# Hash-masked attention and SwiGLU on one core: when the weights are loaded, when two head pairs are hashed, and which engine moves one head's bits

## The chip, the cores and the metric

The kernel runs on one core of a Trainium2 chip, in one launch. The metric is the device time of one execution in microseconds. The time before is the median of three runs; beside it stands one execution taken by the hardware profiler, from which all durations come.

## The reference

Four batches of eight heads, 768 tokens, 64 channels per head. Every query and key is hashed with six projections to six bits; a query sees only the keys with the same six bits. The result goes through an RMS norm and a SwiGLU layer (512 to 1536 to 512 channels).

```python
q_bits = (np.einsum('bhsd,dk->bhsk', q, proj) > 0)
k_bits = (np.einsum('bhsd,dk->bhsk', k, proj) > 0)
mask = q_bucket[:, :, :, None] == k_bucket[:, :, None, :]
scores = np.where(mask, scale * np.matmul(q, k.transpose(0, 1, 3, 2)), -1000000000.0)
attn = softmax(scores); x = attn @ v            # heads side by side: (3072, 512)
xn = x / rms * rms_g
out = (silu(xn @ w_gate) * (xn @ w_val)) @ w_out
```

## The kernel before, in words

**Bits as channels.** A head's queries and keys lie transposed in a tile `QK` with 70 partitions: 64 channels and 6 rows with the hash signs, scaled so that a pair of tokens with equal bits gains a constant that the exp's bias (`EBIAS`) takes off again. So one matmul of 70 rows gives masked scores, and a head's scores cannot start before its six bit rows lie in `QK`.

**Getting a pair of heads ready** (batch 0; `hp` is the pair, `hh` the head in it):

- `load_natural` and `load_v` load q, k and v by DMA from SP's queue (384 KB each).
- `turn_pe` (L141) transposes one head's q or k on TensorE into a PSUM bank `t_ps`; VectorE (DVE) copies it to `qT` or `kT` (L150).
- `cast_pool` (L186, `cast_part` L161) casts both to fp16 into `QK` on GpSimd (POOL).
- `hash_direct` (L230) multiplies with the projections (`d_ps`, L222); `sign` lets DVE write the sign bits of all four tensors of the pair to a tile `bits` (L211); `send` copies them to rows 64 to 69 of `QK` with four DMAs of 9 KB on SP's queue (L251).
- `v_prep` (L277) casts v to fp16 into `vl`; `v_mean` (L290) sums v over the tokens with a matmul (`m_ps`), which DVE scales to `cvb`.

Head pair 0 of batch 0 is prepared in a prologue, its bits written straight to `QK` by DVE.

**Order of the work.** The time is cut into slots. A slot t issues the two score matmuls of the next block (`scores`, L305), the exp of block t on ScalarE (`probs`, L319), and then the functions that a dictionary `plan` lists for slot t, in the order in which they were listed. Three slots make one head for one half of the queries (a unit u: batch u // 2, half u % 2). The heads come in the order (0,0), (0,1), (1,0), (1,1), then heads 2 to 7 of unit 0, then heads 2 to 7 of unit 1, so heads 2 and 4 and 6 of batch 0 start at slots 12, 18 and 24. Each engine runs its instructions in the order of issue; slots hold no engine back, only data does.

```python
    for t in range(LAST):
        if t + 1 < LAST:
            scores(*head_of(t + 1))
        probs(*head_of(t))
        for f in plan[t]:
            f()
```

`av` (L328) multiplies a head's exps with v in two parts; `attn_out` (L344) adds `cvb`, divides (DVE, then POOL's `x` and `sq`), and `sumsq` sums the squares. From slot `TX` = 37 on unit 0 is normed (`norm`, `turn_x`), and from slot 38 `spread` deals out 48 pieces of gate and value matmuls (`feed`, L407 to L415: 12 feature tiles of 128 columns, each gate then value) over slots 38 to 47, and from slot 48 the output projections of the unit before.

**Weights.** `load_w` (L509) loads and casts a piece of a weight matrix with a DMA issued from POOL's queue. Gate and value come in two pieces of 256 input rows each (768 KB in fp16), planned for slots 3 and 7 (gate) and 12 and 16 (value); the output weights follow at slots 39 and 42. All gate and value pieces hold all 1536 columns.

**PSUM.** Three banks (`gps`) are passed round among `t_ps`, `d_ps`, `m_ps`, `x_ps`, `g_ps`, `v_ps` and `y_ps`; scores have two tiles of their own, `o_ps` one. The loads share eight buffers (`lpool`), so a load waits until the tile eight loads before it has been read.

Of the kernel before, what the change touches and what calls it, by code (L numbers as in the profile page):

```python
# [17 lines left out]
S = 768  # L18
D = 64
DMODEL = H * D  # L20
DFF = 1536
# [12 lines left out]
def kernel(  # L34
# [12 lines left out]
    nc = tc.nc  # L47
# [26 lines left out]
    wg = const.tile([128, 4, DFF], FP16, name="wg")  # L74
    wv = const.tile([128, 4, DFF], FP16, name="wv")
# [54 lines left out]
    KROWS = D + 6  # L130
    qT, kT, QK = {}, {}, {}
# [9 lines left out]
    def turn_pe(b, hp, hh, which, keep=nc.vector.tensor_copy, act=()):  # L141

        src = raw[b, hp][0 if which == "q" else 1][:, hh].rearrange(
            "p (j e) d -> p j (e d)", e=2
        )
        ps = bank("t_ps", [128, 3, 128])
        for j in range(3):
            nc.tensor.transpose(ps[:, j, :], src[:, j], ident)  # L148
        psf = ps.rearrange("p j t -> p (j t)")
        keep(turned(b, hp, which)[:, hh, :], psf)  # L150
        o = 0 if which == "q" else S
        for e in act:
            nc.scalar.copy(
                QK[b, 2 * hp + hh, "h"][0:64, o + e * HALF : o + (e + 1) * HALF],
                psf[64 * e : 64 * e + 64, :],
            )

    def turned(b, hp, which):
        return (qT if which == "q" else kT)[b, hp].rearrange("p (h c) -> p h c", h=2)
# [48 lines left out]
    def signs(dst, ps):  # L208

        upper = ps.bitcast(U16).rearrange("p (c two) -> p c two", two=2)[:, :, 1]  # L210
        nc.vector.tensor_scalar(  # L211
            out=dst.bitcast(U16), in0=upper, scalar1=SIGN, scalar2=BIT,
            op0=ALU.bitwise_and, op1=ALU.bitwise_or,
        )

    def hash_pairs(srcs):


        pss = [bank("d_ps", [128, HALF]) for _ in range(2)]
        for t, src in enumerate(srcs):  # L220
            for e in range(2):
                nc.tensor.matmul(  # L222
                    pss[e][32 * t : 32 * t + 32, :],
                    pj[64 * e : 64 * e + 64, 6 * e : 6 * e + 32],
                    src[64 * e : 64 * e + 64],
                    start=True, stop=True, tile_position=(64 * e, 32 * t),
                )
        return pss

    def hash_direct(b, hp, heads):  # L230


        where = [(which, hh) for hh in heads for which in "kq"]
        pss = hash_pairs([turned(b, hp, which)[:, hh, :] for which, hh in where])
        bt = spool.tile([128, S], FP16, name="bits")

        def sign(e):
            signs(bt[:, e * HALF : (e + 1) * HALF], pss[e])

        def direct(which, e):  # L240
            t = where.index((which, heads[0]))
            o = (0 if which == "q" else S) + e * HALF
            signs(
                QK[b, 2 * hp + heads[0], "h"][D:KROWS, o : o + HALF],
                pss[e][32 * t : 32 * t + 6],
            )

        def send():
            for t, (which, hh) in enumerate(where):
                o = 0 if which == "q" else S  # L250
                nc.sync.dma_start(  # L251
                    out=QK[b, 2 * hp + hh, "h"][D:KROWS, o : o + S],
                    in_=bt[32 * t : 32 * t + 6, :],
                )

        return sign, direct, send

    def hash_one(b, hp):

# [45 lines left out]
    def scores(u, i):  # L305
        b, half = divmod(u, 2)
        h, ch = divmod(i, 3)
        ps = scps.tile([128, 2, 512], FP32, name="s_ps")
        for j in range(2):
            jt = 2 * ch + j  # L310
            nc.tensor.matmul(  # L311
                ps[:, j, 0:HALF],
                QK[b, h, "h"][0:KROWS, S + jt * 128 : S + (jt + 1) * 128],
                QK[b, h, "h"][0:KROWS, half * HALF : (half + 1) * HALF],
                start=True, stop=True,
            )
        sps[u, i] = ps
# [183 lines left out]
    def idle(n, new=None):  # L501

        ps = new("z_ps") if new else wz
        for _ in range(n):
            nc.tensor.matmul(ps, zeros16[:, 0:128], zeros16, start=True, stop=True)

    idle(8)

    def load_w(dst, src, kt, n):  # L509
        nc.gpsimd.dma_start(  # L510
            out=dst[:, kt : kt + n, :],
            in_=src[kt * 128 : (kt + n) * 128, :].rearrange("(k p) n -> p k n", p=128),
        )


# [7 lines left out]
    def at(w, s, f, *a):  # L523
        plan[NS * w + s].append(lambda: f(*a))
# [4 lines left out]
    cast_part(0, 0, "k", 1, 0, 1)  # L529
    turn_pe(0, 0, 1, "k")  # L530
    idle(1)
    _, direct, _ = hash_direct(0, 0, (0,))
    turn_pe(0, 0, 1, "q", nc.scalar.copy)
    idle(2)
    for which, e in (("k", 0), ("k", 1), ("q", 0)):
        cast_part(0, 0, which, e, 1, 1)
    for which, e in (("k", 0), ("q", 0), ("k", 1)):
        direct(which, e)
    scores(0, 0)
    _, direct1, _ = hash_direct(0, 0, (1,))  # L540


    def second_head():
# [2 lines left out]
        direct("q", 1)  # L546
        direct1("q", 1)

    pair_signs, sends = {}, {}

    def hash_only(b, hp):
        pair_signs[b, hp], _, sends[b, hp] = hash_direct(b, hp, (0, 1))

    def hash_signs(b, hp):
        for e in range(2):
# [2 lines left out]
    def hash_pair(b, hp):  # L558
        hash_only(b, hp)
        hash_signs(b, hp)  # L560

    def send_pair(b, hp):
        sends[b, hp]()

    at(0, 0, second_head)

    at(0, 1, cast_part, 0, 0, "q", 1, 0, 2, nc.vector)
    for hp, s0 in ((1, 2), (2, 7), (3, 13)):
        at(0, s0, new_pair, 0, hp)
        at(0, s0, turn_pe, 0, hp, 0, "k")  # L570
        at(0, s0 + 1, turn_pe, 0, hp, 1, "k")
        at(0, s0 + 1, cast_pool, 0, hp, "k")
        at(0, s0 + 2, turn_pe, 0, hp, 0, "q")
        at(0, s0 + 3, turn_pe, 0, hp, 1, "q")
        at(0, s0 + 3, cast_pool, 0, hp, "q")
        at(0, s0 + 4, hash_pair, 0, hp)
        at(0, s0 + 5, send_pair, 0, hp)
    at(0, 3, v_prep, 0, 0, nc.vector)
    at(0, 1, load_natural, nc.sync, 0, 3, "k")
    at(0, 1, load_natural, nc.sync, 0, 3, "q")  # L580
    at(0, 2, load_v, nc.sync, 0, 2)
# [1 line left out]
    at(0, 8, v_prep, 0, 1, nc.vector)  # L583
    at(0, 13, v_prep, 0, 2, nc.vector)
    at(0, 19, v_prep, 0, 3, nc.vector)
    for hp, t in enumerate((7, 18, 24, 30)):
        at(0, t, v_mean, 0, hp, 2, range(6))
    for i in range(2):
        at(0, 3 + 4 * i, load_w, wg, moe_w_gate, 2 * i, 2)
        at(0, 12 + 4 * i, load_w, wv, moe_w_val, 2 * i, 2)  # L590
        at(0, 39 + 3 * i, load_w, wo, moe_w_out, 6 * i, 6)


    for hp, ts in ((0, (8, 22, 23, 24, 25, 24, 26, 26, 28, 42)), (1, (12, 27, 28, 29, 30, 29, 41, 32, 33, 43))):
        tl, ts = ts[0], ts[1:]
        for w in "kq":
            at(0, tl, load_natural, nc.sync, 1, hp, w)
        at(0, tl, load_v, nc.sync, 1, hp)
        at(0, ts[0], new_pair, 1, hp)
        for t, hh, w in zip(ts[0:4], (0, 1, 0, 1), "kkqq"):  # L600
            at(0, t, turn_pe, 1, hp, hh, w)
        at(0, ts[4], cast_pool, 1, hp, "k")
        at(0, ts[5], cast_pool, 1, hp, "q")
        if hp == 0:
            at(0, ts[6], hash_pair, 1, hp)
            at(0, ts[7], send_pair, 1, hp)
        at(0, ts[8], v_prep, 1, hp)
        at(0, ts[8], v_sum, 1, hp)

    spots = {  # L610
        (1, 2): (20, (48, 48), (49, 49), 50),
        (1, 3): (45, (57, 57), (58, 59), 60),
        (2, 0): (50, (63, 64, 65, 66), (67, 69, 70, 71), 73),
        (2, 1): (62, (72, 73, 75, 81), (82, 83, 84, 85), 86),
# [16 lines left out]
    at(0, 24, nc.gpsimd.tensor_scalar_mul, gcol, gcol, float(DMODEL) ** 0.5)  # L631
    for n, (u, h) in enumerate(order):
        for part in range(2):
            at(0, 3 * n + 4 + part + (n == 0), av, u, h, part)
        if h % 2:
            if (u, h) == (0, H - 1):

                at(0, 3 * n + 5, o_step, u, h // 2, nc.vector)
                at(0, 3 * n + 5, s_step, u, h // 2)
                at(0, 3 * n + 5, norm_scale, u)  # L640
                at(0, 3 * n + 6, hash_only, 1, 1)
                at(0, 3 * n + 6, hash_signs, 1, 1)
                at(0, 3 * n + 6, norm, u)
                at(0, TX + 1, send_pair, 1, 1)
                at(0, TX - 1, idle, 2, bank)
                at(0, TX, idle, 1, bank)
                for c in range(3):
                    at(0, TX, turn_x, u, c, c == 1)
                continue
            at(0, 3 * n + 5, o_step, u, h // 2)  # L650
            at(0, 3 * n + (10 if h < 7 else 7), s_step, u, h // 2)
# [35 lines left out]
    for u in range(7):  # L687
# [11 lines left out]
        for i in range(9):  # L699
            c, n = divmod(i, 3)  # L700
# [12 lines left out]
    def behind_norm(t):  # L713

        return t - t % NS + 7 if 2 <= t % NS < 7 else t

    for (b, hp), (load, kturns, qturns, _) in spots.items():
# [7 lines left out]
        t = behind_norm(qturns[-1] + 2)  # L725
# [66 lines left out]
```

## Time and profile before

| | us |
|---|---|
| median of 3 runs (lowest to highest) | 349.69 (348.59 to 350.16) |
| the profiled execution | 348.41 |
| its span, first to last instruction | 346.5 |
| TensorE busy (PE) | 331.5 (96%) |
| VectorE busy (DVE) | 233.4 (67%) |
| ScalarE busy (ACT) | 224.3 (65%) |
| GpSimd busy (POOL) | 148.4 (43%) |
| mean granted TensorE clock | 0.99 |

Busy time counts what an engine computes; PEld is TensorE's weight load, which overlaps its matmuls. In the list of slices the span is cut into 40 equal parts of 8.66 us, and a digit is the busy share in tenths; PEclk is the clock that TensorE was granted, in tenths. The chain of waits is followed back from the last instruction, at each step to what released it. "QK<-bits" is the DMA of L251; "SPq" and "POOLq" are the queues from which DMAs are issued. A wait for several things is put down to the one that came last.

### The profile page before, as it was taken

The numbers are of one execution on the slowest core, as the hardware profiler recorded it, in microseconds if no ns is written. First come the engines' busy times: TensorE is split into PE (matmuls) and PEld (weight loads), VectorE is DVE, ScalarE is ACT, GpSimd is POOL, SyncE is SP. The second block draws the span as 40 slices with busy tenths as digits, with TensorE's granted clock in tenths as the row PEclk, the third lists the DMA queues.
The fourth block names the chain that finished last, engine by engine and source line by source line (L and its number), as shares of the span: only waits on it lengthen the run. The fifth ranks groups of instructions, "written<-read, shape, count | busy, mean of one in ns | idle before, by whom it ended". The sixth has DMA issues, their size and how long they took to land.

```text
span 346.5 us, 7807 instructions
## 1 busy us (share of the span) xinstructions
PE 331.5 (96%) x3004; PEld 199.0 (57%) x3004; DVE 233.4 (67%) x489; ACT 224.3 (65%) x325; POOL 148.4 (43%) x202
## 2 busy tenths in 40 slices
PE   8864999999999999999999999999999999999996
PEld 4443575665556646565656556565656556664554
DVE  3855478677688847985688846886586646675770
ACT  2854588666656766777677766777667776863322
POOL 3296272933762373465265533456371121112000
PEclk9999699999999999999999999999999999999999
DMA  7899870980363924443462415300200010001002
GB/s 242 273 187 279 221 138 12 165 153 33 50 153 62 164 75 116 98 66 78 99 136 43 100 65 98 75 3 5 80 17 5 1 62 32 0 2 61 33 0 91
DMA packets 78692, 30.94 MB, mean 89 GB/s; under 512 B 65000, under 2 KB 74688, under 8 KB 78656
## 3 DMA queue, kind: packets, MB, share of 16 engines
q1 hardware_dynamic: 75552, 25.47, 30.2%
q0 software_dynamic: 2656, 4.72, 7.7%
q8 instruction: 23, 0.38, 0.5%
q10 hardware_dynamic: 448, 0.27, 0.3%
q14 instruction: 13, 0.11, 0.1%
HBM read 28.32 MB, written 6.29 MB: 100 GB/s over the span
## 4 chain that ended last, share of the span: by engine, by line
PE 85%; DMA 4%; DVE 3%; ACT 1%; issue 1%; SPq 0%; DVEq 0%
PE v_ps L415 18%; PE g_ps L415 17%; PE y_ps L444 17%; PE s_ps L311 16%; PE o_ps L336 9%; DMA QK<-bits 4%; PE d_ps L202 3%; PE x_ps L398 2%; PE d_ps L222 1%; PE y_ps L463 1%; PE t_ps L148 1%; ACT psb L323 1%; DVE bits L211 1%; PE m_ps L296 1%; DVE a L432 0%
## 5 line engine op out<-in xcount | busy, mean ns | idle before, releaser
L323 ACT ACTIVATE psb<-s_ps,ebias 128x768 f16<-128x768 f32 x192 | 167.8, 899 | 34.4 <-PE s_ps L311 33.4
L311 PE MATMUL s_ps<-QK 70*128 70x384 f16 x384 | 94.7, 328 | 9.4 <-DMA QK<-bits 7.6
L423 ACT ACTIVATE t<-g_ps 128x384 f32<-128x384 f32 x96 | 47.1, 490 | 56.2 <-PE g_ps L415 56.0
L415 PE MATMUL g_ps<-xnT,wg 128*128 128x384 f16 x384 | 82.5, 325 | 0.2
L415 PE MATMUL v_ps<-xnT,wv 128*128 128x384 f16 x384 | 81.7, 325 | 0.2 <-DVE a L432 0.2
L432 DVE SCALAR_TENSOR_TENSOR a<-t,g_ps 128x384 f32<-128x384 f32 x96 | 52.7, 549 | 28.5 <-ACT t L423 27.1
L444 PE MATMUL y_ps<-wo,ht 128*128 128x512 f16 x276 | 68.0, 378 | 0.0
L357 POOL TENSOR_TENSOR x<-otmp,rcp 128x384 f32<-128x384 f32 x31 | 25.7, 829 | 97.3 <-DVE rcp L355 96.9
L336 PEld LDWEIGHTS <-psb 128*128 128x128 f16 x1152 | 52.4, 97 | 19.0 <-issue 4.3
L433 DVE SCALAR_TENSOR_TENSOR ht<-a,v_ps 128x384 f16<-128x384 f32 x96 | 53.2, 554 | 11.3 <-PE v_ps L415 3.1
L311 PEld LDWEIGHTS <-QK 70*128 70x128 f16 x384 | 34.9, 98 | 42.0 <-issue 11.6
L336 PE MATMUL o_ps<-vl,psb 128*128 128x65 f16 x1152 | 56.8, 193 | 0.5 <-DVE vl L280 0.5
L415 PEld LDWEIGHTS <-wv 128*128 128x128 f16 x384 | 35.2, 97 | 22.6 <-issue 1.8
L415 PEld LDWEIGHTS <-wg 128*128 128x128 f16 x384 | 34.7, 97 | 21.2 <-DVE xnT L404 0.6
L444 PEld LDWEIGHTS <-ht 128*128 128x128 f16 x276 | 24.7, 97 | 22.7
L362 POOL TENSOR_TENSOR sq<-x 128x384 f32<-128x384 f32 x31 | 25.6, 826 | 2.4
L194 POOL CAST QK<-kT 64x768 f16<-64x768 f32 x20 | 16.4, 820 | 22.6 <-DVE kT L174 7.7
L456 ACT COPY ysb<-y_ps 128x512 f32<-128x512 f32 x23 | 13.5, 585 | 18.6 <-PE y_ps L444 18.6
L350 DVE TENSOR_TENSOR otmp<-o_ps,cvb 128x390 f32<-128x390 f32 x32 | 17.9, 558 | 10.5 <-PE o_ps L336 10.4
L194 POOL CAST QK<-qT 64x768 f16<-64x768 f32 x20 | 16.5, 825 | 18.5 <-DVE qT L181 17.1
L366 DVE TENSOR_REDUCE ssp<-sq 128x3 f32<-128x384 f32 x32 | 16.9, 528 | 9.9 <-POOL sq L362 9.9
L211 DVE TENSOR_SCALAR bits<-d_ps 128x384 uint16<-128x384 uint16 x20 | 10.7, 553 | 14.2 <-PE d_ps L222 11.5
(70 smaller groups left out, 264.5 us busy)
## 6 DMA issues: line engine op xcount, KB each, us to landing
vn<-in_v_dram SPq DMA_DIRECT2D x16, 384.0 KB
out_dram<-ysb SPq DMA_DIRECT2D x23, 256.0 KB
qL<-in_q_dram SPq DMA_DIRECT2D x40, 96.0 KB
kL<-in_k_dram SPq DMA_DIRECT2D x40, 96.0 KB
kn<-in_k_dram SPq DMA_DIRECT2D x5, 384.0 KB
qn<-in_q_dram SPq DMA_DIRECT2D x5, 384.0 KB
wg<-in_moe_w_gate_dram POOLq DMA_DIRECT2D x2, 768.0 KB, 8.5
wv<-in_moe_w_val_dram POOLq DMA_DIRECT2D x2, 768.0 KB, 9.8
```

The lines of the kernel that those rows point to most:

```text
L194: nc.gpsimd.tensor_copy(QK[b, 2 * hp + hh, "h"][0:64, o : o + S], src[64 * hh : 64 * hh + 64, :])
L311: nc.tensor.matmul(ps[:, j, 0:HALF], QK[b, h, "h"][0:KROWS, S + jt * 128 : S + (jt + 1) * 128], QK[b, h, "h"][0:KROWS, half * HALF : (half ...
L323: nc.scalar.activation(psb[u, h][:, 2 * ch : 2 * ch + 2, :], sps.pop((u, i))[:, :, 0:HALF], AF.Exp, bias=ebias, scale=ESCALE,)
L336: nc.tensor.matmul(o[:, c, hh, 0:65], psb[u, h][:, jt, c * 128 : (c + 1) * 128], vls[b % 2][:, h, 2 * (jt % 3) + jt // 3 if b in PARITY el ...
L350: nc.vector.tensor_add(tmp[:, :, :, 0:65], o[:, :, :, 0:65], cvb[b % 2][:, 2 * hp : 2 * hp + 2, 0:65].unsqueeze(1).to_broadcast([128, 3, 2 ...
L357: eng.tensor_mul(xd.rearrange("p c (h d) -> p c h d", h=2), tmp[:, :, :, 0:64], r.to_broadcast([128, 3, 2, 64]),)
L362: eng.tensor_mul(sq, xd, xd)
L415: nc.tensor.matmul(ps, w[:, kt, fs], xnT[u][:, kt, :], start=(kt == 0), stop=(kt == 3))
L423: nc.scalar.activation(t, fbank[u, ft, "g_ps"], AF.Tanh, scale=0.5)
L432: nc.vector.scalar_tensor_tensor(out=a, in0=t, scalar=1.0, in1=g, op0=ALU.add, op1=ALU.mult)
L433: nc.vector.scalar_tensor_tensor(out=ht[u][:, ft, :], in0=a, scalar=0.5, in1=vv, op0=ALU.mult, op1=ALU.mult)
L444: nc.tensor.matmul(y, ht[u][:, ft, c * 128 : (c + 1) * 128], wo[:, ft, :], start=(ft == 0), stop=(ft == NF - 1),)
```

## The change

- `load_w` takes a range of columns. Gate and value now come in column halves: 768 columns of all 512 input rows, so feature tiles 0 to 5 and 6 to 11. They are planned for slots 20 (gate, first half), 23 (value, first half), 33 and 36.
- Pairs 2 and 3 of batch 0 are turned, cast, hashed and sent from slots 5 and 11 on, before from 7 and 13.
- Of pair 1 (heads 2 and 3) DVE copies head 2's bits to `QK` with two `tensor_copy` of 6 x 768 (`move`); head 3's still go by two DMAs.
- The second query half of pair 0 is cast on POOL at slot 1, before on DVE; v of pair 0 is cast on POOL at slot 1, before on DVE at slot 3. `v_mean` of pair 0 is at slot 4, before 7, and the first head's `av` one slot sooner.
- The loads of batch 1's pair 1 go from slot 12 to 17, those of pair 2 from slot 20 to 34.

```diff
-        def send():
+        def move(hh):
+            for which in "kq":
+                t, o = where.index((which, hh)), 0 if which == "q" else S
+                nc.vector.tensor_copy(
+                    QK[b, 2 * hp + hh, "h"][D:KROWS, o : o + S], bt[32 * t : 32 * t + 6, :]
+                )
+
+        def send(only=heads):
             for t, (which, hh) in enumerate(where):
+                if hh not in only:
+                    continue
                 o = 0 if which == "q" else S
...
-    def load_w(dst, src, kt, n):
+    def load_w(dst, src, kt, n, cols=slice(None)):
         nc.gpsimd.dma_start(
-            out=dst[:, kt : kt + n, :],
-            in_=src[kt * 128 : (kt + n) * 128, :].rearrange("(k p) n -> p k n", p=128),
+            out=dst[:, kt : kt + n, cols],
+            in_=src[kt * 128 : (kt + n) * 128, cols].rearrange("(k p) n -> p k n", p=128),
         )
...
-    at(0, 1, cast_part, 0, 0, "q", 1, 0, 2, nc.vector)
-    for hp, s0 in ((1, 2), (2, 7), (3, 13)):
+    at(0, 1, cast_part, 0, 0, "q", 1)
+    at(0, 1, v_prep, 0, 0)
+    for hp, s0 in ((1, 2), (2, 5), (3, 11)):
...
-        at(0, s0 + 5, send_pair, 0, hp)
-    at(0, 3, v_prep, 0, 0, nc.vector)
+        if hp == 1:
+            at(0, s0 + 5, send_pair, 0, hp, (1,))
+            at(0, s0 + 5, move_head, 0, hp, 0)
+        else:
+            at(0, s0 + 5, send_pair, 0, hp)
...
-    for hp, t in enumerate((7, 18, 24, 30)):
+    for hp, t in enumerate((4, 18, 24, 30)):
         at(0, t, v_mean, 0, hp, 2, range(6))
-    for i in range(2):
-        at(0, 3 + 4 * i, load_w, wg, moe_w_gate, 2 * i, 2)
-        at(0, 12 + 4 * i, load_w, wv, moe_w_val, 2 * i, 2)
+    for i, t in enumerate((20, 33)):
+        cols = slice(i * DFF // 2, (i + 1) * DFF // 2)
+        at(0, t, load_w, wg, moe_w_gate, 0, 4, cols)
+        at(0, t + 3, load_w, wv, moe_w_val, 0, 4, cols)
         at(0, 39 + 3 * i, load_w, wo, moe_w_out, 6 * i, 6)
-    for hp, ts in ((0, (8, ...)), (1, (12, 27, ...))):
+    for hp, ts in ((0, (8, ...)), (1, (17, 27, ...))):
...
-        (1, 2): (20, (48, 48), (49, 49), 50),
+        (1, 2): (34, (48, 48), (49, 49), 50),
...
-            at(0, 3 * n + 4 + part + (n == 0), av, u, h, part)
+            at(0, 3 * n + 4 + part, av, u, h, part)
```

## The prediction

> **What bounds the kernel now.** The page comes first: the slices of the span.
>
> ```profile
> PE   8864999999999999999999999999999999999996
> PEclk9999699999999999999999999999999999999999
> DMA  7899870980363924443462415300200010001002
> ```
>
> From the seventh slice (52 us) on TensorE is full, and its clock is full too; only slices 1 to 5 (8.7 us each) have room. The change edits the plan of slots 0 to 38 (one slot is one block of scores and its exp), and slot 38, the first gate matmul, starts at 58.74 us. So I cost those 58.74 us; the 287.8 us behind them are the same TensorE work in nearly the same order and count at nothing. Next, stretches of those slices:
>
> ```profile
> 17.20:21.80 4.60, 4.56 (x70) 3.71 (x62) 3.67 (x9) 3.34 (x5) 4.38 (x7) 1.00 0.85 161
> 21.80:24.50 2.70, 0.09 (x4) 0.01 (x1) 0.74 (x2) 0.36 (x1) 2.54 (x4) 1.00 1.08 215
> 24.50:30.20 5.70, 5.61 (x76) 3.91 (x76) 3.91 (x9) 4.54 (x6) 2.95 (x5) 1.00 1.06 292
> 30.20:35.10 4.90, 0.00 (x0) 0.00 (x0) 0.62 (x2) 0.45 (x1) 4.68 (x6) 0.82 1.08 254
> 35.10:40.20 5.10, 5.05 (x45) 2.55 (x46) 1.87 (x5) 2.01 (x3) 0.06 (x1) 0.50 1.09 295
> 40.20:58.70 18.50, 17.82 (x243) 12.24 (x240) 14.64 (x32) 16.25 (x23) 9.29 (x12) 1.00 0.42 82
> ```
>
> The columns are length, busy PE, PEld, DVE, ACT, POOL, granted clock, DMA share. TensorE stands still twice while the DMA engines are full, and after the second stop it runs 5 us at half clock. Who is waited for is in the chain of waits of that stretch, and in the list of waits:
>
> ```profile
> 19.51 4.88 DMA QK<-bits
> ...
> 27.73 7.28 DMA QK<-bits
> ...
> 35.95 1.46 PE d_ps L222 x16
> ```
>
> ```profile
> PE s_ps L311 <- DMA QK<-bits: 7.6, 2, 5.0
> ```
>
> The scores of heads 2 and 4 wait 2.63 us (to 24.52) and 4.96 us (to 35.15) for their six rows of hash bits, which L251 copies from SBUF to SBUF by DMA, 9 KB each. The timeline of the issues says why they are late: the gate and value quarters leave POOL's queue at 17.21, 19.86, 25.91 and 34.40, the bits leave SP's at 18.60 and 26.98. In the trace's packet records the first gate quarter (256 rows of 3072 bytes, 247 ns each, 16 on each DMA engine) moves from 18.94 to 23.8, and the first bits move at 22.98; the next bits come out from 33.0 on, behind batch 1's loads and the first value quarter (30.0 to 36.2).
>
> **The change part by part.** *Weights behind the bits* (plan, `load_w`). Until slot 18 no weights are under way. That removes A = 2.63 and B = 4.96, if nothing else is late there. *Clock.* With B goes the half clock. From 35.15 to 39.96 the chain holds 4.81 us of matmuls; the same groups elsewhere in it at full clock: scores 0.48, hash 0.94, o_ps 0.38, then 0.33, 0.35 and 0.33 make 2.81, so C = 2.0. *Value cast and av one slot sooner.* `v_prep` (0,0) goes from DVE (15.14) to POOL, idle from 9.73 to 15.17 (vn had landed by 9.9; the q cast and it are two POOL casts of some 0.83): the 0.49 us that o_ps waits for vl ends, D = 0.5, and DVE loses two casts of 0.56. If that cover went, pair 1's k casts behind them would be late, with 4 us to spare before slot 11. Ceiling: 2.63 + 4.96 + 2.0 + 0.5 = 10.1 us.
>
> *Head 2's bits by DVE.* Two copies of 6 x 768 fp16 replace two DMAs of SP (0.66 to 0.85 us of its queue each). No row shows an fp16 copy inside SBUF; bounds are the 128x128 CAST, 0.23, and the 64x768 CAST, 0.56. I take 0.4, between them (same length as the second, half its bytes). They sit on DVE in front of pair 2's q copies. What is queued: from 10.71 five sign ops (2.76), four t_ps copies of pair 1 (0.51 apart), cvb 0.28, signs 1.02, two moves 0.8, four copies of pair 2: 8.9, to which come waits for turns and hash as before (0.92 + 0.47) and some 0.4 of drain, so pair 2's hash can start at about 21.4 and the scores behind it at 22.5; without the stop TensorE would have been there at 21.9. Head 2 itself is ready near 19.3. *Pairs 2 and 3 two slots sooner.* Same number of turns, casts and hashes; the pace is DVE's. Between the hashes of pairs 2 and 3 DVE has 1.02 + 4 x 0.51 + v_prep 0.56 + ssp 0.54 + otmp and rcp 0.75 = 4.9 us, TensorE 6 x 0.33 + 4 x 0.27 + 4 x 0.33 + 0.94 = 5.3, so here only the copy behind the last turn shows. Together E = 1.3: 0.6 for the first hash and 0.7 for the second, which the second stop hid; bounds 0 (DVE gap-free) and 3.9 (rival 2).
>
> By the Trainium skill (SBUF — State Buffer, "Who interferes with whom") a VectorE copy in a two-port mode and a GpSimd operation exclude each other. The trace agrees: a POOL cast beside the vl cast at 15.14 took 1208 ns instead of 823. By the page alone each move could wait a whole cast.
>
> *Do the later DMAs meet their users?* Pair 2's bits (sent near 23.5) go behind batch 1's first loads, issued after slot 8 (near 20.5, 3 x 384 KB; such a load took about 1.15 us while the queue was alone, before 14 us): landed by 27, wanted near 29. Pair 3's are sent near 30 and wanted from 34. Behind them SP issues pair (1,1)'s loads, now slot 17, near 33; POOL, which nothing holds until its slot, sends the first gate half near 31, when pair 3's casts and x, sq are done. Loads issued beside weights before took 5.5 us (29.92 to 35.42) and 6.85 us (21.64 to 28.49): k lands at 38.5 to 39.9, wanted at 47.63 - 8.4 = 39.2. F = 0.4, bounds 0 and 2.9 (each load alternating with the value half: 16 rows on an engine x (136 + 72 ns) = 3.3 us, q at 44 against 41.1). Pair (1,2)'s load at slot 34 is wanted at slot 48, some 20 us on.
>
> *Column halves.* Two DMAs per matrix, as before, 512 rows of 1536 bytes each instead of 256 of 3072. No record shows such a row: bounds are wo's 1024 bytes, about 100 ns, and 247; I take 136, on the straight line between (nearest is wo's). A half is 512 x 136 / 16 = 4.4 us. The second halves leave POOL behind rstd (ended at 56.08, now 47.7) at 47.7 and 48.5; the slowest weight load took 10.7 us to land, so 59.2. Its user, the value matmul of feature tile 6, ran at 69.64, now 61.2: 2.0 us to spare, no cost. If that cover went, TensorE would stop at once.
>
> Sum: 10.1 - 1.3 - 0.4 = 8.4 us. The profiled execution took 348.41 (span 346.5 and 1.9 around it), so it would take 340.0. The median of the runs, 349.69, stands 1.28 above it; on that footing 341.3, which I predict.
>
> By the Trainium skill (DMA: Bandwidth & Descriptors, "Queues, rings and completion order") a DMA engine drains a packet of typically 9 to 17 descriptors from one queue before it turns to the next. The trace agrees for the bits at 18.60, which came out after 16 rows of the gate quarter; it does not for the large loads, whose rows alternate with weight rows one by one at 0.30 us. For head 7's bits, the last before the gate half, the rule gives 17 x 136 ns = 2.3 us, an estimate, and no cost; a whole half, 4.4 us, would cost 0.5.
>
> **Rivals.** 1. *The weights do not end up behind the bits.* Nothing holds POOL, so the first gate half leaves before pair 3's last bits and the (1,1) loads; a new wait at the bits of head 7 (0.5) and at the (1,1) turns (2.9) takes part of the old. For: POOL's order. Against: the last bits have 4 us. 10.1 - 1.3 - 3.4 = 5.4 gained: 344.3.
>
> 2. *DVE becomes the bound.* Each move waits for a cast of POOL (0.82 twice), costs 0.56 (0.3 more), and pair 3's hash slips 0.7 further: E = 3.9, 5.8 gained: 343.9. For: the 1208 ns; DVE is nearly gap-free from 10.7 to 18.6. Against: POOL has gaps there.
>
> 3. *Slower: the short rows cost what whole rows cost.* At 247 ns a half takes 7.9 us. The (1,1) loads alternate with longer rows (16 x 0.32 = 5.1 us each), F = 3.9. The second halves start to move at 47.7 + 1.9, need 15.8 and about 1.0 beside the head blocks, and land at 66.4, 5.2 after need; such a stop brings the half clock again, 2.0. 10.1 - 1.3 - 3.9 - 5.2 - 2.0 = -2.3: 352.0. Each ns per row costs 0.032 and 0.064 us on these two, so it is level near 222 ns and measurably slower from 240. Against: 1024 bytes took 100.
>
> 4. *No change:* the bits are late whatever goes before them. Against: bits sent at 38.58 came out within half a microsecond of each other once the last value quarter had gone (41.2).
>
> **How the numbers follow.** Forecast 0.63, rival 1 0.14, rival 2 0.11, rival 3 0.08, rival 4 0.04. A measurement tells about 0.5% (1.75 us) from nothing. Forecast and rivals 1 and 2 are faster by more: 0.88; rival 4 is the same, 0.04; rival 3 slower, 0.08. The range runs from the ceiling, 339.6, less 1.0 for the spread of the runs, to rival 1 with as much again and F's bound: 338.6 to 346.0. Left out are rivals 3 and 4 and the ends of the others.
>
> **What would show it.** No wait of s_ps for QK<-bits over 1 us, PEclk full after the start, the first gate matmul near 50.3 us, hash gaps of about 1 us before the scores of slots 11 and 17, gate and value issues at about 31, 35, 48 and 48.5, and the rest 287 to 288 us. Wrong would be: t_ps waiting for kn or qn near 39 (rival 1), DVE without gaps from 10 to 30 with d_ps waiting for it (2), v_ps or g_ps waiting for wv or wg near 61 (3), or the bits' wait still there (4).

## The result, and the profile after

The changed kernel takes 341.0 us (median of four runs, 340.8 to 341.58) against 349.93; ratio 0.9742, 95% interval 0.9692 to 0.9793. A second set of six runs gave 341.29. The profiled execution took 340.80 (span 339.0); the one of before 348.41 (346.5). The slices of the page after:

```profile
PE   7899899999999999999999999999999999999996
PEclk9999999999999999999999999999999999999999
DMA  7942989981809618070826118000200010001002
```

Counted from 1, the two holes of TensorE in slices 3 and 4 (6 and 4 before) are gone, and so is the 6 of the clock in slice 5. The DMA engines, at 9 in slices 3 and 4 before, are now at 4 and 2 there, and busier in slices 7, 11 and 13 (9, 8, 9; before 0, 3, 3). The stretches after (length, busy PE, PEld, DVE, ACT, POOL, clock, DMA share, GB/s):

```profile
15.00:20.00 5.00, 5.00 (x68) 3.27 (x67) 3.75 (x7) 3.64 (x5) 3.70 (x6) 1.00 0.22 76
20.00:25.00 5.00, 5.00 (x59) 2.95 (x58) 4.26 (x9) 3.45 (x5) 4.34 (x6) 1.00 0.74 239
25.00:30.00 5.00, 4.89 (x68) 2.75 (x65) 3.75 (x8) 3.94 (x5) 4.42 (x7) 1.00 0.04 9
30.00:35.00 5.00, 4.63 (x62) 3.46 (x60) 3.15 (x7) 4.96 (x7) 3.87 (x5) 1.00 0.59 77
35.00:40.00 5.00, 4.60 (x62) 3.07 (x60) 3.97 (x9) 3.82 (x6) 3.97 (x7) 1.00 1.12 276
40.00:45.00 5.00, 4.19 (x65) 2.97 (x65) 3.00 (x7) 3.93 (x5) 2.98 (x4) 1.00 1.16 243
```

TensorE is full or nearly so from 15 to 30 us; what it loses now lies between 30 and 45, most of it from 35 on (1.2 us of 10), beside full DMA engines. Who is late there is in the list of waits after (the wait for bits is no longer in it) and in the chain:

```profile
PEld t_ps L148 <- DMA qn<-in_q_dram: 1.1, 1, 1.1
PE t_ps L148 <- DMA qn<-in_q_dram: 0.7, 1, 0.7
PE t_ps L148 <- DMA kn<-in_k_dram: 0.4, 1, 0.4
```

```profile
32.46 8.89 DMA qn<-in_q_dram
41.35 0.04 issue
41.40 0.55 PE t_ps L148 x3
```

Batch 1's second pair of loads is the new wait: q, issued at 32.46, lands 8.9 us later, beside the first gate and value halves.

The first exp starts anywhere from 9.0 to 10.1 us into the span, whichever kernel runs, so the kernels below are compared by the starts of the exps (L323 before, L333 after), counted from that of slot 0, in us:

| kernel | slot 11 | 12 | 17 | 18 | 21 | 28 | 38 |
|---|---|---|---|---|---|---|---|
| before | 11.36 | 15.19 | 19.85 | 26.13 | 30.91 | 37.91 | 48.65 |
| after | 12.84 | 13.64 | 18.93 | 19.73 | 22.08 | 29.03 | 41.38 |
| weights alone (w_late_only) | 11.37 | 12.40 | 17.43 | 18.73 | 22.17 | 29.48 | 40.38 |
| weights early (w_early) | 12.84 | 13.64 | 18.98 | 22.17 | 25.16 | 33.82 | 44.56 |
| turns late (turn_late) | 10.45 | 12.16 | 17.25 | 18.53 | 21.96 | 29.39 | 40.28 |
| bits by DMA (bits_by_dma) | 11.70 | 12.71 | 18.18 | 18.98 | 21.33 | 28.28 | 43.12 |
| loads at 15 (load15) | 12.84 | 13.64 | 18.92 | 19.72 | 22.07 | 29.02 | 39.95 |
| first halves later (w_later) | 12.84 | 13.64 | 18.93 | 19.73 | 22.08 | 29.03 | 40.02 |
| weights, v on POOL (best) | 10.45 | 11.87 | 16.55 | 17.93 | 21.27 | 28.96 | 39.85 |
| loads at 15, bits by DMA (combo) | 11.71 | 12.71 | 18.18 | 18.98 | 21.32 | 28.54 | 39.51 |
| zeros in one stop (warm) | 11.36 | 15.70 | 23.82 | 29.43 | 32.46 | 40.08 | 50.83 |
| zeros in both stops (warm2) | 11.36 | 14.88 | 19.53 | 26.03 | 29.07 | 39.96 | 50.70 |

From slot 38 to the end every one of them takes 287.9 to 288.1 us.

### The profile page after: what moved, and what is told of

Same layout as the page of the kernel before. It is cut to its first block, busy times and chain, and to the rows that moved or that the text cites. A ratio compares the mean times of both kernels' runs of the same rounds, so it can differ in the third digit from the quotient of the medians.

```text
span 339.0 us, 7797 instructions
## 1 busy us (share of the span) xinstructions
PE 330.5 (97%) x3004; PEld 197.4 (58%) x3004; DVE 234.4 (69%) x489; ACT 224.6 (66%) x325; POOL 151.2 (45%) x204
## 4 chain that ended last, share of the span: by engine, by line
PE 90%; DVE 4%; DMA 3%; ACT 2%; issue 1%; POOL 0%; DVEq 0%
PE v_ps L425 18%; PE g_ps L425 18%; PE y_ps L454 17%; PE s_ps L321 17%; PE o_ps L346 9%; PE d_ps L202 3%; DMA qn<-in_q_dram 3%; PE d_ps L222 2%; PE x_ps L408 2%; PE t_ps L148 2%; ACT psb L333 2%; PE z_ps L515 1%; PE y_ps L473 1%; DVE a L442 0%; PE m_ps L306 0%
## 5 line engine op out<-in xcount | busy, mean ns | idle before, releaser
L333 ACT ACTIVATE psb<-s_ps,ebias 128x768 f16<-128x768 f32 x192 | 168.0, 900 | 26.9 <-PE s_ps L321 25.9
L360 DVE TENSOR_TENSOR otmp<-o_ps,cvb 128x390 f32<-128x390 f32 x32 | 17.9, 559 | 10.3 <-PE o_ps L346 10.1
L414 DVE TENSOR_TENSOR xnT<-x_ps,gcol 128x512 f16<-128x512 f16 x22 | 14.5, 685 | 5.8 <-PE x_ps L408 5.8
```

Of the source, the lines that this page charges most:

```text
L333: nc.scalar.activation(psb[u, h][:, 2 * ch : 2 * ch + 2, :], sps.pop((u, i))[:, :, 0:HALF], AF.Exp, bias=ebias, scale=ESCALE,)
L360: nc.vector.tensor_add(tmp[:, :, :, 0:65], o[:, :, :, 0:65], cvb[b % 2][:, 2 * hp : 2 * hp + 2, 0:65].unsqueeze(1).to_broadcast([128, 3, 2 ...
```

## The experiments

**Weights early.** The kernel after with the four old weight loads.

```diff
-    for i, t in enumerate((20, 33)):
-        ...  # column halves at t and t + 3
+    for i in range(2):
+        at(0, 3 + 4 * i, load_w, wg, moe_w_gate, 2 * i, 2)
+        at(0, 12 + 4 * i, load_w, wv, moe_w_val, 2 * i, 2)
```

> The kernel after, with gate and value in four quarters of 256 rows at slots 3, 7, 12 and 16, as before. Theory (bits stuck behind weights are the loss): weights move again from about 18 us; head 2 does not wait, since DVE copies its bits; head 3's DMA and above all pair 2's come out late, a wait of s_ps for bits of 1 to 4 us returns at slot 14 or 18, while the wait of t_ps for batch 1's loads at slots 28 to 30 goes: 342 to 346. Rival (the earlier turns and the DVE copies did it, the place of the weights is idle): 341, no wait for bits over 0.5 us.

345.14 us (342.87 to 346.54), ratio 0.9852 (0.9778 to 0.9926). The wait for pair 2's bits is back, from the list of waits and the chain of this kernel:

```profile
PE s_ps L321 <- DMA QK<-bits: 2.4, 1, 2.4
```

```profile
24.26 6.93 DMA QK<-bits
...
34.16 0.64 PE s_ps L321 x2
34.80 0.49 PE o_ps L346 x9
```

The scores of slot 18 wait 2.4 us, and behind them matmuls again take twice their time (0.64 for scores that take 0.33). t_ps waits for no load. So the other edits without the weights are worth 4.1 us at slot 38 (48.65 - 44.56): the first stop is gone, since DVE copies head 2's bits (slot 12 at 13.64 against 15.19), and sending pair 2 sooner halves its wait, no more.

**Weights alone.** The kernel before, `load_w` with columns, halves at slots 20, 23, 33 and 36; nothing else.

> The kernel before, with only the weights moved: column halves at slots 20, 23, 33 and 36. Theory: both waits for bits and the half clock go without any other edit; the hash waits on DVE that the second stop hid come up (about 2 us), batch 1's loads keep slot 12 and go ahead of the weights: 341 to 343. Rival (pairs 2 and 3 must also be turned sooner, or head 2's bits moved by DVE): a wait of 2 us or more for bits stays at slot 12 or 18, 345 or more.

339.71 us (339.15 to 340.69), ratio 0.9706 (0.9650 to 0.9763): the whole gain. The intervals do not part it from the full change; by the starts, one profiled execution each, slot 38 comes 1.00 sooner than in the kernel after. Its list of waits holds what is left of the 7.6 us:

```profile
PE s_ps L311 <- DMA QK<-bits: 0.3, 1, 0.3
```

and in the stretches of the old stops TensorE works (same columns):

```profile
21.80:24.50 2.70, 2.64 (x40) 1.62 (x31) 1.52 (x4) 1.77 (x3) 2.56 (x4) 1.00 0.92 309
30.20:35.10 4.90, 4.24 (x59) 3.19 (x58) 3.20 (x7) 4.48 (x7) 4.69 (x6) 1.00 0.60 124
```

The first of them stood at 0.09 of 2.70 before, the second at 0. The rival is out: neither the sooner turns nor the copies by DVE are needed. Place and shape of the weights change together here, and no run changes one alone. That the place does it is argued from the issues: the bits of pairs 1 and 2 leave SP from 17.73 to 26.45, and the first gate half, of whatever shape, leaves POOL at 31.80.

**Bits by DMA.** The kernel after with all four of pair 1's bits sent by SP.

```diff
-        if hp == 1:
-            at(0, s0 + 5, send_pair, 0, hp, (1,))
-            at(0, s0 + 5, move_head, 0, hp, 0)
-        else:
-            at(0, s0 + 5, send_pair, 0, hp)
+        at(0, s0 + 5, send_pair, 0, hp)
```

> The kernel after, with all four tensors of pair 1 sent by DMA again, no copies by DVE. Theory (the copies cost DVE time in front of pair 2's hash and save nothing once the weights are away): bits of head 2 land near 21, wanted at 22; the gap before slot 11, 2.46 us, shrinks by up to 1: 340 to 341. Rival (the copies are needed): a wait of s_ps for bits at slot 12 of 1 us or more, 342 or more.

340.36 us (339.75 to 343.77), ratio 0.9711 (0.9646 to 0.9776). Slot 11 comes 1.14 us sooner than in the kernel after (11.70 against 12.84) and no wait for bits appears; the copies were not needed. Its profiled execution was the slowest of the five, 343.77: t_ps waited 0.77 us for kn and 1.28 for qn, and half clock followed, so slot 38 is late there.

**Turns late.** Pairs 2 and 3 from slots 7 and 13 again, the rest as after.

```diff
-    for hp, s0 in ((1, 2), (2, 5), (3, 11)):
+    for hp, s0 in ((1, 2), (2, 7), (3, 13)):
```

> The kernel after, with pairs 2 and 3 turned from slots 7 and 13 on, as before. Theory (two slots sooner is reserve, not gain, once the weights are away): DVE's queue is spread more evenly, the bits of pair 3 are sent two slots later, near 32, and meet the first gate half, so a wait at slot 24 of 0 to 3 us; 340.5 to 344. Rival (the sooner turns carry the gain): waits for bits at slots 18 and 24 of 3 us or more together, 345 or more.

340.16 us (339.71 to 341.45), ratio 0.9722 (0.9664 to 0.9780). Waits for bits add up to 0.4 us. At slot 28 it is 0.36 behind the kernel after (29.39 against 29.03), at slot 38 1.10 ahead: pair 3's bits are now behind the (1,1) loads, which SP issues at 26.79, 5.2 us before the first gate half, and t_ps does not wait. The sooner turns gain nothing that lasts.

**Loads at 15; first halves later.** Two ways to part the (1,1) loads from the weights.

```diff
-    ... (1, (17, 27, 28, ...
+    ... (1, (15, 27, 28, ...
```

```diff
-    for i, t in enumerate((20, 33)):      # gate at t, value at t + 3
+    for i, ts in enumerate(((25, 26), (33, 36))):
```

> The kernel after, with batch 1 pair 1's three loads at slot 15 instead of 17, so that SP issues them before pair 3's bits and some 5 us before the first gate half. Theory (the remaining loss of 1.5 us at slots 28 to 31 is these loads queued beside the gate half): t_ps no longer waits for kn or qn, the steps of slots 29 and 31 go back to 0.80 and 0.87 us, slot 38 comes 1.4 us sooner, 339.6. Rival (the loads are late for another reason, or pair 3's bits, now behind them, take the wait over): a wait of 1 us or more stays, 341.

> The kernel after, with the first gate and value halves at slots 25 and 26 instead of 20 and 23, the loads of batch 1 at their places. Theory (the weights' first half is what the (1,1) loads queue beside): no wait of t_ps for kn or qn; the gate matmul's weights land about 50, so a wait of g_ps or v_ps of 0 to 1 us may come: 339.5 to 340.5. Rival (SP issues the loads too late whatever the weights do): t_ps waits as before, 341.

339.86 us (339.37 to 340.46), ratio 0.9707 (0.9679 to 0.9736), and 339.81 (339.08 to 340.27), ratio 0.9697 (0.9659 to 0.9735). In both t_ps waits for no load and slot 38 comes 1.43 and 1.36 us sooner than in the kernel after. The stretches of loads at 15 that answer to the kernel after's:

```profile
35.00:40.00 5.00, 5.00 (x70) 3.52 (x67) 3.93 (x9) 4.17 (x6) 4.23 (x6) 1.00 1.16 209
40.00:45.00 5.00, 4.88 (x76) 3.33 (x75) 4.25 (x10) 4.85 (x7) 3.24 (x4) 1.00 0.56 99
```

Moving the load or moving the weights has the same effect, so it is their meeting that costs, not either alone. In the second, both halves leave POOL at 37.7 and 38.7 and gate and value still wait for no weights.

**Half clock.** Matmuls of zeros in the stops of the kernel before.

```diff
         for f in plan[t]:
             f()
+        if t in (10, 16):                 # warm: only 16, with 20
+            idle({10: 11, 16: 21}[t], bank)
```

> The kernel before with 20 matmuls of zeros (512 columns, 0.22 us each at full clock) added on TensorE behind slot 16, in front of the scores that wait for pair 2's bits; the output does not change. Theory (the half clock behind the second stop costs 2.0 us by itself): the wait for the bits ends at the same time, the clock stays full, the steps of slots 19 and 20 shrink from 2.65 and 1.29, span 1.5 to 2 shorter, 347.9. Rival (the half clock hides beside ScalarE and costs nothing of its own): 349 to 350.

350.8 us (349.86 to 352.29), ratio 1.0024 (1.0001 to 1.0048): no difference that counts. In its profile the half clock fell on the first stop (24.1 to 34.4 us), where there were no zeros, so its total does not test the second; slots 18 to 21, at full clock, need 3.03 us.

> The kernel before with matmuls of zeros on TensorE in both stops: 11 behind slot 10, 21 behind slot 16; the output does not change. Theory (the half clock costs 1.7 to 2.0 us by itself): the clock stays full through both stops, the steps of slots 19 and 20 shrink from 2.65 and 1.29 to about 1.85 and 0.80, and the time falls to 348. Rival (it hides beside ScalarE): 349 to 350 with a full clock.

350.86 us (350.17 to 351.84), ratio 1.0055 (1.0026 to 1.0084): half a per cent slower. Yet the clock did what was wanted:

```profile
30.00:35.00 5.00, 4.59 (x23) 1.84 (x19) 0.70 (x2) 0.52 (x1) 4.73 (x6) 1.00 1.08 257
35.00:40.00 5.00, 4.19 (x59) 2.40 (x60) 2.87 (x7) 3.32 (x5) 0.04 (x1) 1.00 1.09 299
40.00:45.00 5.00, 2.64 (x30) 2.14 (x30) 1.23 (x3) 2.55 (x4) 1.73 (x3) 0.92 0.70 123
```

From slot 18 to 21 it needs 3.04 us instead of 4.78: the half clock cost 1.74 us. But with those won, the scores of slot 24 come before pair 3's bits, which lie behind the second value quarter; a new wait of 2.25 us and a new half clock (the 0.92) take more than was won. The theory was right on the clock and wrong on the time: alone, a full clock there is worth nothing while the weights stay in front.

**Versions from these.** `best` is weights alone with pair 0's casts on POOL, v_mean at slot 4 and the first av a slot sooner; `combo` is the kernel after with bits by DMA and loads at 15; beside it the kernel after once more.

> The kernel before with the weights in column halves at slots 20, 23, 33 and 36, and with pair 0's casts on POOL, v_mean at slot 4 and the first av one slot sooner; pairs 2 and 3, the loads of batch 1 and the bits by DMA as before. Theory (the later weights carry the gain, and the half microsecond at the first av adds to it): 339.2 to 339.7, faster than the kernel after by 1.3 to 1.8. Rival (the half microsecond is taken back at pair 2's hash, which waits for DVE): as with the weights alone, 339.7 to 340.

> The kernel after without the copies by DVE (all of pair 1's bits by DMA) and with batch 1 pair 1's loads at slot 15. Theory (the copies cost 1.1 us in front of pair 2's hash, the loads beside the gate half 1.4): both losses go; measured from the first exp, slot 38 comes at 39.2 us instead of 41.4, median about 338.8, 2.2 below the kernel after. Rival (one of the two is taken back by a wait for pair 1's or pair 3's bits): 339.5 to 340.

> The kernel after, unchanged, on the same chip as its variant without copies and with sooner loads. Every theory: 340.8 to 341.6; the wait of t_ps for kn and qn differs from execution to execution by up to 1 us.

`best` 339.52 us (338.61 to 339.67), ratio 0.9690 (0.9661 to 0.9719); `combo` 339.29 (338.94 to 339.71), ratio 0.9715 (0.9671 to 0.9759), 2.0 below the kernel after's 341.29 (340.67 to 341.71) on the same chip. `combo` beats the kernel after on one chip; `best` ran on another, and its interval (to 0.9719) ends just below that of the kernel after's second set (from 0.9728). Between the two the runs don't decide. `best` is 0.92 us ahead of weights alone at slot 10 and 0.53 at slot 12 and at slot 38; what is lost goes at slot 12, and its waits for bits add up to 0.9 us against 0.3.

## Why the prediction was right, point by point

Forecast 341.3, measured 341.0; the range and the way were right, and so was the mechanism: with the weights behind the bits both stops and the half clock go, and with the weights in their old places a stop and the half clock come back. Of the signs, the waits, the clock and the issues came (30.64, 34.36, 48.3 and 49.1); the first gate matmul starts at 51.09 instead of 50.3. By its terms, with the starts of the table:

| term | forecast | measured | from |
|---|---|---|---|
| A, stop for head 2's bits | 2.63 | 2.79 | slot 12, before less weights alone |
| B, stop for head 4's bits | 4.96 | 4.98 | step to slot 18: 6.28 before, 1.30 weights alone |
| C, half clock | 2.0 | 1.74 | slots 18 to 21, before less zeros in both stops |
| D, first av | 0.5 | 0.53 | in two other kernels: slot 38, weights alone less best |
| E, DVE in front of the hashes | -1.3 | -1.16 | not measured: what A to D (10.04) leave over at slot 28 (8.88 gained) |
| F, batch 1's loads beside the weights | -0.4 | -1.42 | slots 28 to 38: 12.35 after, 10.93 loads at 15 |

Together 7.46 of 7.27 at slot 38, with E fitted; 0.19 stay open, of which 0.16 is the longer step to slot 38 itself. The span fell 7.5, since the first exp came 0.37 sooner by chance and the stretch behind slot 38 took 0.16 more.

**What failed is F**, mis-sized: 1.4 instead of 0.4, within its bound of 2.9, and in it the load of q. My 0.4 was for k, and k cost 0.45: the step to slot 29 is 1.25, with loads at 15 0.80. q I had late at the far bound alone, so it stood in the sum at nothing; it took 8.9 us to land and cost the other 0.97 (steps to slots 30 and 31: 2.77 against 1.80). I had priced the loads by rows in which they took 5.5 and 6.85 us to land. The packet records of the kernel after show two things on top of each other. The loads, issued from 31.91 on, move their first row only at 36.16, when 381 of the gate half's 512 rows have gone; with the first halves later the first row moves 1.1 us after the issue. And from 38.62 on, after a pause of 0.7 us, the value half's rows take turns with those of q and v, as my far bound had it. That is rival 1 at half price, in its place: t_ps waits for kn near 39 and for qn at 41. Its other half, head 7's bits, cost nothing, though the last of their four DMAs, issued at 31.20, moved only at 35.24, behind the same gate rows.

**The near hit hides this.** On the footing of the profiled execution I had 340.0, and it took 340.80: 7.6 us gained of a forecast 8.4. The medians fell by 8.9, and that they come near the forecast is luck. The runs of before spread over several microseconds, and the spread goes with their granted clock: in the three sets run beside the experiments, those at a clock of 0.995, 0.99, 0.985 and 0.98 took 347.2, 348.5, 350.0 and 351.1 us (medians), while the kernel after is at 1.00 in all ten of its runs. C was worked out from an execution at 0.99; runs at a lower clock lose more than that, and win it back. The sum has no term for this, and whether it is the whole difference of 1.3 is not shown.

**E** came out in sum, but the runs do not bear out its reason. Weights alone, without copies and sooner turns, leaves over nearly as much at slot 28 (A, B and C give 9.51, 8.43 are gained). The share of the copies is measured: without them (bits by DMA) slot 11 comes 1.14 sooner and slot 28 0.75. And of the hash gaps that I had put at about 1 us, that before slot 11 is 1.66 and that before slot 17 1.16 (steps of 2.46 and 1.96 against 0.80 before). The two copies took more than the 0.8 us I gave them.

```profile
L252 DVE COPY QK<-bits x2: 352/618/885, 18.7 to 19.1; 6x768 f16<-6x768 f16 x2
```

This row of the trace (shortest, median, longest in ns) has one copy of 352 and one of 885. The second starts at 19.08 while a POOL cast runs (18.75 to 19.76) and ends 0.2 us behind it; two other profiles show 352 and 882, 353 and 883. By the Trainium skill (SBUF — State Buffer, "Who interferes with whom") a VectorE copy in a two-port mode and a GpSimd instruction exclude each other; the trace agrees. With turns late, where no cast runs beside them, both copies take 0.35, and that lies between my bounds. Rival 2 came true for one of the two copies.

**Rival 3** fell by its price: rows of 1536 bytes took 134 ns (median of 2048; 136 was estimated), and the second halves landed without g_ps or v_ps waiting. **Rival 4** fell with the waits.

What the forecast did not ask is whether the weights need the other parts. It gave the gain to the weights and priced the rest as small costs and one small gain; but weights alone gain 8.27 at slot 38, one more than the whole change (7.27), and of the rest only D helps (0.5), while the copies cost 1.1 at slot 11 and the (1,1) loads at slot 17 cost 1.4.

## What to carry to other kernels

When a 9 KB transfer is late, look at what was put into the DMA engines before it, and move the bulk whose user is far off; here that alone was worth about ten microseconds of 350 (ratio 0.9706). Then ask of every other edit in the change whether it still gains once that is done, and try the part alone. A load is to be priced by what was issued just ahead of it and by everything that will be in flight until it lands; and taking away one stop pays only up to the next thing that was late behind it.

## What the runs showed of the hardware that was not expected

Half clock follows stops that are much shorter than the 5 us of before, and can set in after them: with weights early a wait of 2.4 us ended at 31.33, and the clock was halved from 32.8 for 6.8 us; with bits by DMA waits of 0.8 and 1.3 us were followed by 3.4 us of half clock from 42.0; in the kernel after, waits of 0.4 and 0.7 us (1.1 counted at the weight load) had none. The Trainium skill (TensorE: Matmul & The Clock Gate, "HAM oscillation — how this bites in real kernels") gives gaps over about 3.4 us as the ones to avoid; these runs differ, and shorter ones are not safe. Where the half clock falls also changes between kernels with the same stop: behind the first stop, of 2.6 to 2.8 us, the kernel before shows none and the kernel with zeros in one stop 10.2 us.

The traces show what decides it. In every trace that lists the clock, its changes lie a whole number of steps of 3.41 us apart: 8 steps full and then 2 at half before, 5 and 3 with zeros in one stop, 11 and 1 with bits by DMA. Cut in these steps, the first stop of before (first two rows) lies across two; the second fills one (third row):

```profile
19.75:23.16 3.41, 2.10 (x29) 1.61 (x27) 2.63 (x6) 2.41 (x3) 3.21 (x5) 1.00 0.94 183
23.16:26.57 3.41, 2.05 (x31) 0.94 (x32) 0.64 (x2) 0.91 (x2) 3.27 (x5) 1.00 1.09 227
29.98:33.40 3.42, 0.21 (x7) 0.08 (x3) 0.84 (x2) 0.67 (x1) 3.20 (x5) 1.00 1.10 241
```

TensorE is idle for 1.3, 1.4 and 3.2 us of them, and half clock begins behind the third alone. With zeros in one stop, most of the first stop falls into one step:

```profile
20.72:24.13 3.41, 1.31 (x17) 0.91 (x14) 1.97 (x5) 1.62 (x2) 3.14 (x5) 1.00 1.06 200
```

It is idle for 2.1 us, and half clock follows. Over the twelve traces (all but that of `best`) half clock began behind every step at full clock with 1.64 us idle or more and behind none with 1.51 or less. So what counts in these traces is the idle time summed in such a step, and a stop of 2 to 3 us costs half clock or not by where it falls. One step at half clock takes 0.005 off the mean clock of 346.5 us (3.41 / 2 / 346.5), so by that count the runs of before, at 0.995 to 0.98, hold one to four of them. What ends the half clock is not shown: it lasted one, two or three steps.
